# Fused attention and two expert layers: converted weight blocks used in place, q and k loads issued later, three small moves at the start

## Chip, cores and metric

One Trainium2 chip, one of its cores. The metric is the device time of one execution in microseconds (us), the median of three runs.

## The reference

Three stages follow each other: attention with a soft cap on the scores, a dense layer with a squared ReLU, and a top-1 expert layer.

```python
# q, k, v: (2 batches, 12 heads, 448 rows, 64), float32
s = q @ k.T / 8;  s = cap * tanh(s / cap);  a = exp(s - max) / (sum + 1e-9);  x = a @ v
# x becomes (896, 768); w_in (768, 2048) and w_out (2048, 768) are float64
x = relu(x @ w_in) ** 2 @ w_out
# 8 experts, w1 (8, 768, 1024), w2 (8, 1024, 768), float32
e = argmax(xn @ en.T / tau);  out = gate[e] * (relu(x @ w1[e]) @ w2[e])
```

## The kernel before

**Number format.** Every float32 operand of a big product is split into a high part in a reduced format and a low rest: `qh` and `ql` of a query, `kp` (both parts of a key stacked on the 128 partitions), `xh` and `xl` of the activations, `wh` and `wl` of a weight block. The dense layer then takes three products per block (lines 554 to 556).

**Attention.** The 24 heads are taken in pairs, m = 0 to 11. One pair is seven blocks of 128 keys: three of its first head, one that holds the last 64 keys of both, three of its second head. Two blocks make a group g. TensorE computes the scores `sc` of group g + 2 (line 423), ScalarE makes `p_t` of them by a tanh and an exponential (lines 425 and 426), and TensorE multiplies `p_t` of group g with the values (`pv`, line 444). Values lie in three rotating tiles `vt0`, `vt1`, `vt2` and, for the shared block, in `vs0` or `vs1`. A pair's result is divided on VectorE (`rs`, `rows`, lines 463 to 467), transposed on TensorE (`xp`, line 483), and split into `xh` (ScalarE) and `xl` (VectorE).

**Front of a head.** `turn(n)` transposes the loaded q and k of head n on VectorE into `tq`. `split_k` and `split_q` make `kp`, `qh` and `ql` of it; `ql` and the upper half of `qh` are GpSimd's. `front_first` is the same for head 0. `load_heads` loads q and k for the next pair with four transfers into `qk`, of which there are two; it is called in `turn` of each odd head, right behind the transpose that frees the tile.

**Weights.** w_in and w_out arrive as pairs of 32-bit words. A block's raw words are loaded into `wr` (768 KB, three buffers), scaled into `wf` (384 KB, four buffers) and patched with shifts (`narrow`, lines 205 to 208), then split into `wh` and `wl`. The first four blocks of w_in (NPRE) are converted during the attention of the first batch, by `convert_early`, one step of VectorE per group. Each is then stored to a buffer `wk` in DRAM, since the second batch reads all blocks there, and the first batch's dense layer loads it back from there (line 218) as block 0 to 3. Blocks 4 and on are scaled by ScalarE (line 222).

**Order.** All of it is one written order per engine. Loads, stores and reloads of the weights, q, k and v go through SyncE's queue (SP) alone, in program order; a transfer there also waits, as the program is built, for a transfer that stands some eight places before it. After the first batch's attention, mlp(0) is interleaved with the attention of the second batch.

Of the kernel before, what the change touches and what calls it, by code (L numbers as in the profile page):

```python
# [13 lines left out]
ALU = mybir.AluOpType  # L14
# [6 lines left out]
def kernel(  # L21
# [27 lines left out]
    nc = tc.nc  # L49
    f32 = lambda ap: ap.bitcast(F32)  # L50

    B, H, S, D = q.shape
# [3 lines left out]
    P = 128  # L56
# [35 lines left out]
    def load_heads():  # L92

        n = nload[0]
        if n >= len(order):
            return
        k_ = 1 if n < 2 else 2
        nload[0] = n + k_
        b, h = order[n]
        if n % 2 == 0:  # L100
            raw["tile"] = ap.tile([P, 2, S // SQ, SQ], F32, tag="qk", name=f"qk{n}", bufs=2)
        qk = raw["tile"][:, n % 2:n % 2 + k_].rearrange("p h s d -> p (h s) d")
        for i, a in enumerate((k, q)):
            halves = a[b].rearrange("h s d -> (h s) d")[h * S:(h + k_) * S].rearrange(
                "(s t) (j d) -> j t s d", t=SQ, d=SQ)
            for j in range(2):
                e = nc.scalar if n == 0 and j else nc.sync
                o = (2 * (1 - i) + j) * SQ
                e.dma_start(qk[o:o + SQ], halves[j])
        for i in range(k_):  # L110
            raw[n + i] = raw["tile"][:, n % 2 + i]

    def load_v(n, e=nc.sync):
        b, h = order[n]
        i = n % 2
        e.dma_start(vt[n % 3][:, :, :D], v[b, h, i * D:i * D + KS].rearrange("(c p) d -> p c d", p=P))
# [8 lines left out]


    capb = const.tile([P, 1], F32, name="capb")
    nc.scalar.dma_start(capb, cap.to_broadcast([P, 1]))
    load_v(0, nc.scalar)
    taub = const.tile([P, 1], F32, name="taub")  # L130

# [22 lines left out]
    def scale():  # L154
        nc.vector.reciprocal(rcap, capb)
        nc.vector.tensor_scalar_mul(rcap, rcap, 1.0 / (D ** 0.5))
# [18 lines left out]
    chunks = []  # L175
# [8 lines left out]
    def add_chunk(src, a, w, wide=False, keep=None, extra=False):  # L184
        chunks.append(dict(src=src, a=a, w=w, wide=wide, keep=keep, extra=extra))

    def w_tile(tag, n, c, bufs, dt=F32R):
        pool = extra_pool[n % 2] or wp
        bufs = bufs if pool is wp else 2
        t = pool.tile([P, WMAX], dt, tag=tag, name=f"{tag}{n}", bufs=bufs)  # L190
        return t[:, :c["a"] * c["w"]].rearrange("p (a w) -> p a w", a=c["a"])

    def raw_w(c, n):
        c["raw"] = ap.tile([P, 2 * WMAX], I32, tag="wr", name=f"wr{n}", bufs=3)[:, :2 * c["a"] * c["w"]].rearrange(
            "p (a w) -> p a w", a=c["a"])
        nc.sync.dma_start(c["raw"], c["src"]())
        c["parts"] = c["raw"].rearrange("p a (w t) -> p a w t", t=2)
# [14 lines left out]
    def w_stage(stage, n):  # L212

        c = chunks[n]

        def load():
            c["f"] = w_tile("wf", n, c, 4, F32)
            nc.sync.dma_start(c["f"], c["src"]())

        def scaled():  # L220
            c["f"] = w_tile("wf", n, c, 4, F32)
            nc.scalar.mul(c["f"], c["parts"][:, :, :, 1].bitcast(F32), 2.0 ** -112)
            c["narrow"] = narrow(c)

        def hi():
            c["hi"] = w_tile("wh", n, c, 4)
            if eng["hi"] == "act":
                nc.scalar.copy(c["hi"], c["f"])  # L228
            else:
                nc.vector.tensor_copy(c["hi"], c["f"])  # L230

        def lo():
            c["lo"] = w_tile("wl", n, c, 4)
            nc.vector.tensor_tensor(c["lo"], c["f"], f32(c["hi"]), op=ALU.subtract)  # L234

        if stage == "load" and c["wide"]:
            return [lambda: raw_w(c, n)]
        if stage == "conv0":
            return [scaled if c["wide"] else load]
        if stage == "conv1" and c["wide"]:  # L240
            return [lambda i=i: c["narrow"][i]() for i in range(3)]
        if stage == "store" and c["keep"] is not None:
            return [lambda: nc.sync.dma_start(c["keep"](), c["f"])]
        if stage == "split":
            return [hi, lo]
        return []
# [50 lines left out]
    early = []  # L297

    def convert_early():

        def first(i):
            c = early[i]
            c["f"] = w_tile("wf", 1000 + i, c, 4, F32)
            nc.vector.tensor_scalar_mul(c["f"], c["parts"][:, :, :, 1].bitcast(F32), 2.0 ** -112)
            c["narrow"] = narrow(c)

        def last(i):
            c = early[i]
            c["narrow"][2]()
            nc.sync.dma_start(c["keep"](), c["f"])  # L310
            if i + 2 < len(early):
                raw_w(early[i + 2], 1002 + i)

        for i in range(len(early)):
            yield first(i)
            yield early[i]["narrow"][0]()
            yield early[i]["narrow"][1]()
            yield last(i)

    def add_mlp_chunks(b):  # L320
        off = 0
        blocks = [(0, f, 0, NCC) for f in range(NF)]
        blocks += [(1, d, a, 4) for d in range(NCC) for a in range(0, NF, 4)]
        for m, col, a0, n in blocks:
            o = off

            def given(m=m, col=col, a0=a0, n=n):
                return w_src[m][a0 * P:(a0 + n) * P, col * P * wm:(col + 1) * P * wm].rearrange(
                    "(a p) w -> p a w", p=P)

            def kept(o=o, n=n):
                return wk[0][:, o:o + n * P].rearrange("p (a w) -> p a w", a=n)

            if not wide:
                add_chunk(given, n, P)
            elif b == 0 and m == 0 and col < NPRE:
                early.append(dict(src=given, a=n, w=P, keep=kept))
                add_chunk(kept, n, P)
            elif b == 0:
                add_chunk(given, n, P, True, kept)  # L340
            else:
                add_chunk(kept, n, P)
            off += n * P

    for b in range(B):
        add_mlp_chunks(b)
# [11 lines left out]
    def attention():  # L358
# [5 lines left out]
        def turn(n):  # L364

            qk = raw.pop(n)
            tq = ap.tile([P, S], F32, tag="tq", name=f"tq{n}", bufs=2)
            nc.vector.transpose(tq, qk.rearrange("p s d -> p (s d)"))
            if n % 2:
                load_heads()  # L370
            kp = ap.tile([P, S + D], F32R, tag="kp", name=f"kp{n}", bufs=3)
            i = n % 2
            nc.gpsimd.memset(f32(kp[:, :D] if i else kp[:, S:]), 0.0)
            qh = ap.tile([P, S], F32R, tag="qh", name=f"qh{n}", bufs=3)
            st[n] = (kp, qh, qlo[n % 3])
            front[n] = tq, kp[:, i * D:i * D + S], qh, qlo[n % 3]
# [7 lines left out]
        def split_q(n):  # L384

            tq, _, qh, ql = front[n]
            copy(qh[:D], tq[:D])
            nc.gpsimd.tensor_copy(qh[D:], tq[:D])
            nc.gpsimd.tensor_tensor(ql[D:], tq[:D], f32(qh[:D]), op=ALU.subtract)  # L389

        def front_first():

            turn(0)
            tq, keys, qh, ql = front[0]
            nc.scalar.copy(keys[D:], tq[D:])
            nc.vector.tensor_copy(qh[:D], tq[:D])
            nc.scalar.copy(qh[D:], tq[:D])
            nc.vector.tensor_tensor(keys[:D], tq[D:], f32(keys[D:]), op=ALU.subtract)  # L398
            nc.gpsimd.tensor_tensor(ql[D:], tq[:D], f32(qh[:D]), op=ALU.subtract)

        def copy(o, i):
            if eng["kh"] == "dve":
                nc.vector.tensor_copy(o, i)
            else:
                nc.scalar.copy(o, i)  # L405
# [81 lines left out]
        def fronts(g):  # L487

            for m, i in blocks[2 * g:2 * g + 2]:
                n = 2 * m + 2 + (i > 3)  # L490
                if i == 0 and n < N and not m:
                    turn(n)
                if i in (1, 5) and n < N:
                    split_k(n)
                    yield
                if i in (2, 6) and n < N:
                    split_q(n)
                    if n + 1 < N:
                        turn(n + 1)
                    yield  # L500
# [4 lines left out]

        todo, late, front = [], [], {}
        conv = convert_early()
        front_first()
        turn(1)
        scale()  # L510
        split_q(1)
        split_k(1)
        scores(0)
# [671 lines left out]
```

## Time and profile before

| | us |
|---|---|
| three runs | 522.92, 524.54, 525.24 |
| median | 524.54 |
| the profiled execution's own time | 524.37 |
| its span, first to last instruction | 522.6 |

| engine | busy us | share of the span |
|---|---|---|
| TensorE (PE) | 506.6 | 97% |
| VectorE (DVE) | 369.8 | 71% |
| ScalarE (ACT) | 283.2 | 54% |
| GpSimd (POOL) | 60.3 | 12% |

The span lies 1.77 us below the profiled execution's time; the rest lies around the instructions. All times in the rows below count from the start of the span. The first batch's attention fills about the first 77 us, mlp(0) with the second batch's attention goes to about 243 us, and what follows is mlp(1) and the experts.

### The profile page before, as it was taken

To read this page: it belongs to the slowest core of one execution; us is meant where nothing else is said; L and a number is where in the kernel's file an instruction comes from. 1 tells how busy PE (TensorE), PEld (TensorE's weight loads), DVE (VectorE), ACT (ScalarE), POOL (GpSimd) and SP (SyncE) were. 2 spreads that over 40 slices of the span, in tenths; PEclk is the share of its full clock that TensorE was granted. 3 is DMA by queue.
4 is the path that set the end of the run, shared out by engine and by line. 5 is a ranking of instruction groups with operands and counts; after the bars stand their busy time and mean duration, and the time that the engine had idled before them with its cause. 6 is when DMAs were issued, how large, how long until landed. Compare 5 with 4: busy or idle time off the path is not lost.

```text
span 522.6 us, 8325 instructions
## 1 busy us (share of the span) xinstructions
PE 506.6 (97%) x2898; PEld 464.4 (89%) x2898; DVE 369.8 (71%) x713; ACT 283.2 (54%) x521; POOL 60.3 (12%) x102
## 2 busy tenths in 40 slices
PE   7999979999999999999999999999999999999995
PEld 5899969999999999999998999999899898998993
DVE  6799969899998989765597476555358344446662
ACT  5978858687966787764244242222362323445531
POOL 5554431111120110002000000000000000000000
PEclk9999979999999999999999999999999999999998
DMA  8887996968855778765433123435512345544651
GB/s 123 191 170 172 226 259 187 232 202 268 207 180 181 222 237 249 229 208 155 159 117 121 43 74 110 135 124 153 156 44 78 108 137 170 184 156 151 213 151 40
DMA packets 129597, 85.19 MB, mean 163 GB/s; under 512 B 59010, under 2 KB 116226, under 8 KB 129552
## 3 DMA queue, kind: packets, MB, share of 16 engines
q1 hardware_dynamic: 119920, 79.07, 54.2%
q10 hardware_dynamic: 9536, 5.52, 4.0%
q8 instruction: 24, 0.39, 0.3%
q14 instruction: 21, 0.17, 0.1%
q0 software_dynamic: 96, 0.04, 0.0%
HBM read 66.68 MB, written 18.28 MB: 163 GB/s over the span
## 4 chain that ended last, share of the span: by engine, by line
PE 89%; DMA 5%; SPq 1%; DVE 1%; issue 1%; POOL 1%; ACT 0%; DVEq 0%; POOLq 0%; ACTq 0%
PE pv L444 9%; PE h L554 8%; PE y L554 8%; PE h L556 8%; PE h L555 7%; PE y L556 7%; PE y L555 7%; PE sc L423 5%; PE z L554 4%; PE e L554 4%; PE e L555 4%; PE z L556 4%; PE e L556 4%; PE z L555 4%; DMA vs<-in_v_dram 2%; DMA vt<-in_v_dram 2%
## 5 line engine op out<-in xcount | busy, mean ns | idle before, releaser
L234 DVE TENSOR_TENSOR wl<-wf,wh 128x512 fp32r<-128x512 f32 (+1 forms) x140 | 114.5, 830 | 48.1 <-ACT wh L228 46.8
L228 ACT CAST wh<-wf 128x512 fp32r<-128x512 f32 (+1 forms) x97 | 65.7, 697 | 20.4 <-PE z L556 8.8
L554 PE MATMUL y<-gh,wh 128*128 128x448 f32 x192 | 72.4, 377 | 0.0
L554 PE MATMUL h<-xh,wh 128*128 128x448 f32 x192 | 72.0, 375 | 0.0
L556 PE MATMUL h<-xl,wh 128*128 128x448 f32 x192 | 70.4, 367 | 0.0
L555 PE MATMUL h<-xh,wl 128*128 128x448 f32 x192 | 70.3, 366 | 0.0
L556 PE MATMUL y<-gl,wh 128*128 128x448 f32 x192 | 70.2, 366 | 0.0
L555 PE MATMUL y<-gh,wl 128*128 128x448 f32 x192 | 70.1, 365 | 0.0
L444 PEld LDWEIGHTS pv<-vt,p_t 128*112 128x112 f32 x576 | 64.4, 181 | 5.9 <-issue 4.1
L444 PE MATMUL pv<-vt,p_t 128*112 128x65 f32 x576 | 63.6, 262 | 3.8 <-DMA vt<-in_v_dram 3.8
L425 ACT ACTIVATE p_t<-sc,rcap 128x448 f32<-128x448 f32 x84 | 49.1, 631 | 21.5 <-PE sc L423 19.4
L426 ACT ACTIVATE p_t<-p_t,capb 128x896 f32<-128x896 f32 x42 | 43.9, 1045 | 1.4
L389 POOL TENSOR_TENSOR ql<-tq,qh 64x448 fp32r<-64x448 f32 x23 | 27.5, 1197 | 132.0 <-ACT qh L405 93.6
L584 ACT ACTIVATE r<-h 128x448 f32<-128x448 f32 x32 | 17.3, 540 | 45.0 <-PE h L556 32.4
L423 PE MATMUL sc<-qh,kp 128*128 128x448 f32 x96 | 37.2, 388 | 2.5 <-DVE kp L398 1.2
L230 DVE CAST wh<-wf 128x512 fp32r<-128x512 f32 (+1 forms) x43 | 21.9, 509 | 24.5 <-PE y L556 19.8
L556 PEld LDWEIGHTS h<-xl,wh 128*128 128x128 f32 x192 | 36.2, 188 | 3.1
L554 PEld LDWEIGHTS h<-xh,wh 128*128 128x128 f32 x192 | 36.3, 189 | 2.8
L556 PEld LDWEIGHTS y<-gl,wh 128*128 128x128 f32 x192 | 36.1, 188 | 3.0
L555 PEld LDWEIGHTS h<-xh,wl 128*128 128x128 f32 x192 | 36.3, 189 | 2.7
L555 PEld LDWEIGHTS y<-gh,wl 128*128 128x128 f32 x192 | 36.2, 188 | 2.5
L554 PEld LDWEIGHTS y<-gh,wh 128*128 128x128 f32 x192 | 36.1, 188 | 2.5
(239 smaller groups left out, 936.7 us busy)
## 6 DMA issues: line engine op xcount, KB each, us to landing
wr<-in_moe_w_in_dram SPq DMA_DIRECT2D x16, 768.0 KB, 5.4
wr<-in_moe_w_out_dram SPq DMA_DIRECT2D x24, 512.0 KB, 4.2
wf<-in_moe_w_dram SPq DMA_DIRECT2D x24, 384.0 KB, 3.5
wf<-in_moe_w_dram SPq DMA_DIRECT2D x36, 256.0 KB, 3.1
wf<-wk SPq DMA_DIRECT2D x20, 384.0 KB, 3.6
wk<-wf SPq DMA_DIRECT2D x16, 384.0 KB, 5.3
wk<-wf SPq DMA_DIRECT2D x24, 256.0 KB, 4.3
wf<-wk SPq DMA_DIRECT2D x24, 256.0 KB, 2.9
```

The lines of the kernel that those rows point to most:

```text
L228: nc.scalar.copy(c["hi"], c["f"])
L230: nc.vector.tensor_copy(c["hi"], c["f"])
L234: nc.vector.tensor_tensor(c["lo"], c["f"], f32(c["hi"]), op=ALU.subtract)
L389: nc.gpsimd.tensor_tensor(ql[D:], tq[:D], f32(qh[:D]), op=ALU.subtract)
L423: nc.tensor.matmul(sc[:, :S], h[0][:, c * P:(c + 1) * P], h[x], start=t == parts[0][0] and x == 1, stop=t == parts[-1][0] and x == 2)
L425: nc.scalar.activation(p_t[:, j], sc[:, :S], AF.Tanh, scale=rcap)
L426: nc.scalar.activation(p_t, p_t, AF.Exp, scale=capb)
L444: nc.tensor.matmul(o, w, x, start=i == 0 and t % 2 == 0, stop=i == NK - 1, skip_group_check=True)
L554: nc.tensor.matmul(o, wh, xh, start=first, stop=False)
L555: nc.tensor.matmul(o, wl, xh, start=False, stop=False)
L556: nc.tensor.matmul(o, wh, xl, start=False, stop=last)
L584: nc.scalar.activation(r, o[:, :S], AF.Relu)
```

## The change

Four things change; nothing else in the kernel does.

1. Blocks 0 to 3 take the converted tile `wf` as it lies (`taken`); their four reloads from `wk` are gone. Their stores to `wk` stay, each now issued one step later.
2. `load_heads` is called in block 6 of a pair, behind `split_q`, where it was in block 2 behind the transpose. The raw block that is fetched during the conversion is fetched at other steps.
3. The transfer of `cap` goes from ScalarE's queue to GpSimd's, and the two small operations of `scale` stand first on VectorE.
4. `ql` of head 0, and the upper half of `qh` of head 1, go from GpSimd to VectorE.

```diff
-    nc.scalar.dma_start(capb, cap.to_broadcast([P, 1]))
+    nc.gpsimd.dma_start(capb, cap.to_broadcast([P, 1]))
...
+        def taken():
+            c["f"] = c["early"]["f"]
+
+        if "early" in c and stage in ("load", "conv0"):
+            return [taken] if stage == "conv0" else []
...
-        def last(i):
-            c = early[i]
-            c["narrow"][2]()
-            nc.sync.dma_start(c["keep"](), c["f"])
-            if i + 2 < len(early):
-                raw_w(early[i + 2], 1002 + i)
+        def fetch(i):
+            if i < len(early):
+                raw_w(early[i], 1000 + i)
 
         for i in range(len(early)):
             yield first(i)
+            if i > 1:
+                fetch(i + 1)
             yield early[i]["narrow"][0]()
             yield early[i]["narrow"][1]()
-            yield last(i)
+            early[i]["narrow"][2]()
+            if not i:
+                fetch(2)
+            yield
+            nc.sync.dma_start(early[i]["keep"](), early[i]["f"])
...
-                add_chunk(kept, n, P)
+                add_chunk(None, n, P)
+                chunks[-1]["early"] = early[-1]
...
             nc.vector.transpose(tq, qk.rearrange("p s d -> p (s d)"))
-            if n % 2:
-                load_heads()
...
-            nc.gpsimd.tensor_copy(qh[D:], tq[:D])
+            (nc.gpsimd if n > 1 else nc.vector).tensor_copy(qh[D:], tq[:D])
...
-            nc.gpsimd.tensor_tensor(ql[D:], tq[:D], f32(qh[:D]), op=ALU.subtract)
+            nc.vector.tensor_tensor(ql[D:], tq[:D], f32(qh[:D]), op=ALU.subtract)
...
                     split_q(n)
+                    if i == 6:
+                        load_heads()
                     if n + 1 < N:
                         turn(n + 1)
...
+        scale()
         front_first()
         turn(1)
-        scale()
+        load_heads()
         split_q(1)
```

The order of instructions on TensorE does not change, and ScalarE's loses only the transfer. On VectorE the first rows change, those of heads 0 and 1. Before:

```order
L135 MEMSET zero_99 128x448
L368 STREAM_TRANSPOSE tq0_147<-qk0_86 128x448
L396 CAST qh0_151<-tq0_147 64x448
L398 TENSOR_TENSOR kp0_149<-tq0_147,kp0_149 64x448
L368 STREAM_TRANSPOSE tq1_157<-qk0_86 128x448
L155 RECIPROCAL rcap_134<-capb_95 128x1
L156 TENSOR_SCALAR rcap_134<-rcap_134 128x1
L403 CAST qh1_166<-tq1_157 64x448
L403 CAST kp1_164<-tq1_157 64x448
L382 TENSOR_TENSOR kp1_164<-tq1_157,kp1_164 64x448
L368 STREAM_TRANSPOSE tq2_196<-qk2_137 128x448
```

The same place on VectorE in the changed kernel:

```order
L135 MEMSET zero_99 128x448
L155 RECIPROCAL rcap_134<-capb_95 128x1
L156 TENSOR_SCALAR rcap_134<-rcap_134 128x1
L377 STREAM_TRANSPOSE tq0_149<-qk0_86 128x448
L403 CAST qh0_153<-tq0_149 64x448
L405 TENSOR_TENSOR kp0_151<-tq0_149,kp0_151 64x448
L406 TENSOR_TENSOR ql0_119<-tq0_149,qh0_153 64x448
L377 STREAM_TRANSPOSE tq1_159<-qk0_86 128x448
L410 CAST qh1_163<-tq1_159 64x448
L395 CAST qh1_163<-tq1_159 64x448
L410 CAST kp1_161<-tq1_159 64x448
L389 TENSOR_TENSOR kp1_161<-tq1_159,kp1_161 64x448
```

The two operations on `rcap` moved ahead of the first transpose, and `ql0` and the second part of `qh1` came over from GpSimd.

On SyncE's queue, in the program's order, this stands behind the first pairs' loads before the change (the number right behind `qk`, `vt` and `vs` is the head or tile, `wr1000` is the raw form of block 0):

```order
L109 DMA qk4_159<-in_k_dram 32x28x32 x2
L109 DMA qk4_159<-in_q_dram 32x28x32 x2
L109 DMA qk6_208<-in_k_dram 32x28x32 x2
L109 DMA qk6_208<-in_q_dram 32x28x32 x2
L116 DMA vt2_83<-in_v_dram 128x3x64
L196 DMA wr1000_217<-in_moe_w_in_dram 128x6x256
L196 DMA wr1001_219<-in_moe_w_in_dram 128x6x256
L121 DMA vs1_85<-in_v_dram 64x64 x2
L116 DMA vt0_81<-in_v_dram 128x3x64
```

And this in the changed kernel:

```order
L109 DMA qk4_164<-in_k_dram 32x28x32 x2
L109 DMA qk4_164<-in_q_dram 32x28x32 x2
L116 DMA vt2_83<-in_v_dram 128x3x64
L196 DMA wr1000_212<-in_moe_w_in_dram 128x6x256
L196 DMA wr1001_214<-in_moe_w_in_dram 128x6x256
L109 DMA qk6_255<-in_k_dram 32x28x32 x2
L109 DMA qk6_255<-in_q_dram 32x28x32 x2
L121 DMA vs1_85<-in_v_dram 64x64 x2
L116 DMA vt0_81<-in_v_dram 128x3x64
```

The four transfers of q and k for heads 6 and 7 moved behind the two raw blocks.

The second place on the same queue is the end of the first batch's attention. Before:

```order
L116 DMA vt2_83<-in_v_dram 128x3x64
L196 DMA wr4_743<-in_moe_w_in_dram 128x6x256
L218 DMA wf1_745<-wk_136 128x768
L109 DMA qk16_766<-in_k_dram 32x28x32 x2
L109 DMA qk16_766<-in_q_dram 32x28x32 x2
L196 DMA wr5_806<-in_moe_w_in_dram 128x6x256
L218 DMA wf2_808<-wk_136 128x768
L310 DMA wk_136<-wf1003_712 128x768
L116 DMA vt0_81<-in_v_dram 128x3x64
L121 DMA vs0_84<-in_v_dram 64x64 x2
L196 DMA wr6_849<-in_moe_w_in_dram 128x6x256
L218 DMA wf3_861<-wk_136 128x768
```

And in the changed kernel:

```order
L116 DMA vt2_83<-in_v_dram 128x3x64
L196 DMA wr4_741<-in_moe_w_in_dram 128x6x256
L196 DMA wr5_797<-in_moe_w_in_dram 128x6x256
L109 DMA qk16_821<-in_k_dram 32x28x32 x2
L109 DMA qk16_821<-in_q_dram 32x28x32 x2
L116 DMA vt0_81<-in_v_dram 128x3x64
L121 DMA vs0_84<-in_v_dram 64x64 x2
L196 DMA wr6_842<-in_moe_w_in_dram 128x6x256
L326 DMA wk_136<-wf1003_705 128x768
```

The reloads `wf1`, `wf2`, `wf3` are gone, `wr5` moved ahead of the four transfers of q and k, and the store of block 3 moved from ahead of `vt0` to behind it.

## Rows read from the trace of the kernel before

**Rows 1.** TensorE's waits, 5 to 75 us: total us, times, longest.

```profile
PE pv L444 <- DMA vt<-in_v_dram: 3.8, 1, 3.8
PE pv L444 <- DMA vs<-in_v_dram: 1.6, 1, 1.6
```

**Rows 2.** Stretches: length, busy PE, PEld, DVE, ACT, POOL, PEclk, DMA share, GB/s.

```profile
26.00:69.50 43.50, 42.50 (x346) 40.80 (x346) 42.32 (x79) 36.28 (x51) 21.87 (x28) 1.00 0.91 200
69.50:73.30 3.80, 0.05 (x1) 0.08 (x1) 3.61 (x9) 2.32 (x4) 1.70 (x2) 0.79 0.93 301
73.30:78.50 5.20, 5.20 (x24) 5.06 (x25) 0.69 (x2) 1.91 (x3) 0.00 (x0) 0.50 1.01 184
...
100.00:243.00 143.00, 143.00 (x866) 133.50 (x865) 124.11 (x214) 106.25 (x199) 16.85 (x30) 1.00 0.73 217
```

**Rows 3.** Timeline of TensorE, end of the first attention: start, duration, instruction.

```profile
76.26 0.95 PE L483 MATMUL xp<-ident,rows 112*128 112x112 f32 x4
```

**Rows 4.** Timeline of VectorE, the same place.

```profile
68.20 0.63 DVE L368 STREAM_TRANSPOSE tq<-qk 128x448 f32<-128x448 f32 x1
...
71.44 0.76 DVE L467 TENSOR_TENSOR rows<-pv,rs 112x256 f32<-112x256 f32 x2
...
72.66 0.62 DVE L382 TENSOR_TENSOR kp<-tq,kp 64x448 fp32r<-64x448 f32 x1
77.81 0.62 DVE L485 TENSOR_TENSOR xl<-xp,xh 128x448 fp32r<-128x448 f32 x1 [4.54 <-ACT xh L484]
```

**Rows 5.** Timeline of SyncE's queue, the same place.

```profile
63.21 0.74 SPq L196 DMA_DIRECT2D wr<-in_moe_w_in_dram  x1
...
64.72 0.38 SPq L310 DMA_DIRECT2D wk<-wf  x1
65.19 0.38 SPq L116 DMA_DIRECT2D vt<-in_v_dram  x1
```

**Rows 6.** The chain that ended last, near 65 us: start, length, what.

```profile
65.19 7.92 DMA vt<-in_v_dram
```

**Rows 7.** Timeline of all engines, the first 12 us.

```profile
4.57 0.65 DVE L368 STREAM_TRANSPOSE tq<-qk 128x448 f32<-128x448 f32 x1 [3.16 <-DMA qk<-in_q_dram]
...
5.79 1.12 POOL L399 TENSOR_TENSOR ql<-tq,qh 64x448 fp32r<-64x448 f32 x1 [1.89 <-DVE qh L396]
...
5.84 1.55 DVE L398 TENSOR_TENSOR kp<-tq,kp 64x448 fp32r<-64x448 f32 x1 [0.21 <-ACT kp L395]
...
9.30 1.45 DVE L382 TENSOR_TENSOR kp<-tq,kp 64x448 fp32r<-64x448 f32 x1
...
10.77 0.65 DVE L368 STREAM_TRANSPOSE tq<-qk 128x448 f32<-128x448 f32 x1
```

**Rows 8.** Timeline of all engines, 20 to 23 us.

```profile
20.02 1.69 PE L444 MATMUL pv<-vt,p_t 128*112 128x65 f32 x16
...
22.19 0.56 DVE L304 TENSOR_SCALAR wf<-wr 128x768 f32<-128x768 f32 x1 [2.42 <-DMA wr<-in_moe_w_in_dram]
...
22.67 0.35 DVE L463 TENSOR_SCALAR rs<-pv,ecap 112x4 f32<-112x4 f32 x2
```

**Rows 9.** Timeline of SyncE's queue, 10 to 27 us.

```profile
10.03 1.21 SPq L109 DMA_DIRECT2D qk<-in_q_dram  x2
...
16.63 1.07 SPq L196 DMA_DIRECT2D wr<-in_moe_w_in_dram  x2
...
19.99 2.74 SPq L109 DMA_DIRECT2D qk<-in_k_dram  x2
22.78 4.10 SPq L109 DMA_DIRECT2D qk<-in_q_dram  x2
```

**Rows 10.** Transfers by line: issues, KB each, median us from issue to landing.

```profile
qk<-in_q_dram SPq DMA_DIRECT2D x22, 112.0 KB, 3.8
...
taub<-in_moe_tau_dram ACTq DMA_DIRECT2D x1, 0.5 KB, 5.9
xg<-x2d,ixu POOLq DMA_INDIRECT x1, 3.1
```

## The prediction

> **What bounds the kernel now.** I read the stretches first, then TensorE's waits, then the timelines at the places that the two name.
>
> From 100 to 243 us TensorE is busy throughout at full clock, VectorE 124.11 of 143 us [rows 2]. There a change of loads is worth nothing by itself; what counts is how early TensorE gets there. Before that the stretches show two things. From 26 to 69.5 us TensorE has 42.50 of 43.50 us and VectorE 42.32: both are full, and neither can go ahead of the other for long. Then comes a hole: from 69.5 to 73.3 us TensorE does nothing, and from 73.3 to 78.5 us it works at a granted clock of 0.50, the 1.2 GHz level, where the rows around show 1.00, the 2.4 GHz level [rows 2].
>
> The waits say what made the hole: `pv` stood 3.8 us for a load of `vt`, the longest wait of the attention; the next one, 1.6 us for `vs`, lies near 25 us [rows 1]. The chain of waits shows that load: issued at 65.19 us, 7.92 us until it has landed [rows 6]. SyncE wasn't late with it. Just ahead in its queue stand a raw block (768 KB, 63.21 us), a reload of a converted block (384 KB) and a store (384 KB, 64.72 us) [rows 5], and the load landed behind them.
>
> So the hole costs 3.8 us of standing and, at half clock, half of the 5.2 us after it, 2.6 us: 6.4 us in all.
>
> **The hole.** The change takes the three reloads `wf1` to `wf3` from this place and a fourth one ahead of it, moves the store behind `vt0`, and puts both raw blocks, `wr4` and `wr5`, ahead of the four transfers of q and k. `vt0` then has 1.5 MB of raw blocks ahead, as much as today in all, but they needn't wait for a transpose any more and can be under way earlier. `vt0` itself can't be issued before TensorE's last read of the tile. That lies three groups ahead of the use at 69.5 us; a group is 2.5 us (8.8 us a pair, below), with its own reading some 9 us: 60.5 us on today's clock, 59 with the advance below. So its issue lies between 59 and today's 65.19, and I take 60, near the lower end, as what stood ahead of it is gone or earlier. Even with the 7.92 us of now it lands at 68. TensorE will want it at 69.5 − 2.4 = 67.1 (below), so it is at worst 0.9 us late, and that hides in the next wait. I take the wait as gone.
>
> **What is late next.** Behind this `pv` TensorE transposes `rows` (`xp`), and VectorE writes them at 71.44 to 72.20 us [rows 4]. VectorE didn't stand in the hole, it caught up. So `xp`, now at 76.26 us [rows 3], can't come before 72.25 on today's clock of VectorE: 76.26 − 72.25 = 4.0 us, not 6.4. From `xp` to 78.5 us are 2.24 us at half clock, of which 1.1 come back if the clock stays up. The stand that is left, about 2 us, is near the 1.6 us at `vs`, after which the clock stands at 1.00 [rows 1, 2], and further from 3.8. VectorE then no longer stands 4.54 us for `xh` [rows 4], so it moves up with TensorE.
>
> **VectorE's own advance.** The hole's new end moves with VectorE, so what VectorE gains ahead counts in full. Two places:
>
> *The start.* The low part of key 0 takes 1.55 us beside GpSimd's `ql` of 1.12 us, that of key 1 1.45 us, where the same operation takes 0.62 elsewhere [rows 4, 7]. With `ql0` on VectorE (about 0.65, like that 0.62) the first drops to 0.62; the second still meets GpSimd's `ql1`, at about 0.85. The upper half of `qh1` adds 0.4; the two operations of `scale` leave their place behind the second transpose (0.3) and go where VectorE waits 3.16 us for q [rows 7]. Sum: −0.93 + 0.65 − 0.6 + 0.4 − 0.3 = −0.8 us up to the transpose at 10.77. Bounds: if the contention stays, −0.93 and −0.6 fall away and it is +0.75.
>
> *The first raw block.* VectorE waits 2.42 us for it until 22.19 us [rows 8]; it was issued at 16.63, behind q and k of heads 6 and 7, which wait for a transpose. SyncE has nothing to do from 11.24 us on [rows 9], and now `vt2` and the raw blocks stand next: issue at about 12, landing 4.6 us earlier, at 17.6, ahead of VectorE, which is free at 22.19 − 2.42 − 0.8 = 19.0. It then stands for TensorE instead: the `pv` at 20.02 lasts 1.69 us [rows 8], less 0.8 gives 20.9 for `rs`, which is at 22.67 now. The advance is 1.7 us from there on (about 2.4 + 0.8 if nothing stood in the way, 0.8 if the block came no earlier).
>
> TensorE's 1.6 us at `vs` goes too, as `vs1` is issued some 2 us earlier behind raw blocks 4.6 us earlier. That gives nothing more: VectorE sets the pace, and TensorE's lead of 2.4 us turns into the stand before `xp`.
>
> **Edits at nothing.** `cap`: the nearest rows are 3.1 us from issue to landing for the one gather on GpSimd's queue and 5.9 us for `tau`, a load of the same size [rows 10]. GpSimd can issue it near 0.8 us; I take 3.1, landing at 3.9, hidden behind q at 4.57, as it is the row of that queue. At 5.9 it would be 6.7, and VectorE's first transpose would start at 7.0: 2.4 us lost. The stores one step later, the raw block fetched at another step: nobody waits for them within a group. Taking the tile in place adds no instruction; ScalarE needs the tile again only for block 4, after VectorE has split block 0.
>
> **Sum.** 1.7 + 4.0 + 1.1 = 6.8 us against the profiled execution's 524.37 us: 517.6 us. That execution is 0.17 us below the median, which I neglect. The 1.77 us around the span stay.
>
> **Rivals.**
>
> *TensorE isn't held by VectorE.* If the timeline slides together better than I read it, the whole 6.4 come back, and TensorE's 0.8 + 1.6: 8.8 us, 515.6. For it: VectorE's durations vary with what GpSimd does beside them. Against: 42.32 of 43.50 [rows 2].
>
> *The hole moves and stays.* `vt0` still stands behind 1.5 MB of raw blocks. If it is late by more than the 2 us that VectorE allows, TensorE stands as long as now and the clock falls again. Then only the 1.7 us of advance are left: 522.7, no change that can be told. For it: `vt` took 7.92 us behind 1.5 MB. Against: the earlier issue.
>
> *`cap` comes late.* VectorE's first row waits for it. By the 5.9 us above: 517.6 + 2.4 = 520.0. The Trainium skill speaks for this one (SBUF — State Buffer, section "SBUF: two separate sides"): descriptors of a transfer issued by GpSimd are written through the port pair that it shares with VectorE, and such a transfer went from about 620 to about 3100 ns beside a VectorE copy. No run here shows it yet; in the first microseconds VectorE has one memset.
>
> *q and k come late (slower).* A pair of heads takes, by the transposes of heads 2 and 15, (68.20 − 10.77) ÷ 13 × 2 = 8.8 us [rows 4, 7]. The loads had 11 of 7 blocks from call to transpose, 13.9 us, and now have 7, 8.8 us. Behind the two raw blocks, the load of now was issued from 19.99 to 26.88 us [rows 9] and lands 3.8 us later [rows 10]: 10.7 us. If each of the five pairs up to the hole took that, VectorE would wait 1.9 us five times, 9.5 us: 517.6 + 9.5 = 527.1. It is slower than now from 1.4 us late each. Against: one pair alone stands behind two raw blocks in the new order, and the 6.9 us of issuing were spent waiting for transfers that will have landed earlier. The Trainium skill bears on it (DMA: Bandwidth & Descriptors, section "Queues, rings and completion order"): each DMA engine takes a queue's descriptors in order, so small loads behind big ones wait; the `vt` load agrees, at 7.92 us behind 1.5 MB [rows 5, 6].
>
> **Chances and range.** Forecast 0.56; TensorE free 0.15; hole stays 0.14; `cap` late 0.08; q and k late 0.06; 0.01 for the rest. About 0.5%, 2.6 us, is what a measurement of this kernel can tell from no change. Faster than that: the forecast, the first and the third rival, and a quarter of the second, 0.83; same 0.11; slower 0.06. The range runs from just under the free TensorE, 515.0, to 522.0, which takes in the late `cap` and a hole that stays in part. Alone, the forecast would have 516 to 519.
>
> **What would show it.** In the profile after: no wait of TensorE near 67 us over 2.5 us; granted clock 1.00 from 12 us to 243 us; `xp` before block 0's first matmul held by `rows` of VectorE; no wait of VectorE for a raw block; `rcap` written before the first transpose, which starts at 4.6; the transpose of head 2 near 10.0; the mlp's first matmul 6 to 7 us earlier. I am wrong if VectorE waits for q and k at any of the transposes, if `vt` or `vs` still holds TensorE long enough for 0.50 to show up, or if the lead is lost between 100 and 243 us.

## The result, and the profile after

The changed kernel takes 518.33 us (median of 5 executions, 517.87 to 520.11) against 524.54 us (522.92 to 525.32): a ratio of 0.9899, 95% interval 0.987 to 0.9927. Six more executions of it gave 518.25 us, 0.9878 (0.9851 to 0.9904). Predicted were 517.6 us. The profiled execution took 517.91 us, 6.46 less than the profiled one of before (524.37), with a span of 516.2 us.

The stretches, with the columns of [rows 2]:

```profile
26.00:66.00 40.00, 40.00 (x331) 38.82 (x330) 39.00 (x75) 35.44 (x51) 20.41 (x26) 1.00 0.86 181
66.00:70.00 4.00, 3.30 (x30) 2.92 (x29) 3.93 (x8) 3.93 (x6) 2.85 (x3) 1.00 0.46 72
70.00:74.00 4.00, 3.75 (x23) 3.35 (x22) 3.83 (x9) 2.82 (x6) 0.00 (x0) 1.00 0.95 306
74.00:78.00 4.00, 4.00 (x29) 3.76 (x29) 4.00 (x5) 4.00 (x7) 1.60 (x2) 1.00 0.24 35
...
100.00:243.00 143.00, 143.00 (x862) 133.36 (x861) 121.08 (x208) 105.58 (x202) 17.19 (x30) 1.00 0.76 218
```

The hole is gone: TensorE loses 0.7 us between 66 and 70 us and 0.25 behind it, and the granted clock stays at 1.00, where [rows 2] have 3.75 us of standing and 5.2 us at 0.50. TensorE's waits from 3 to 100 us say the same (columns as in [rows 1]):

```profile
PE sc L430 <- DVE kp L389: 1.5, 1, 1.5
...
PE pv L451 <- DMA vt<-in_v_dram: 0.7, 1, 0.7
PE xp L490 <- DVE rows L474: 0.2, 1, 0.2
```

The 3.8 us for `vt` are 0.7, the 1.6 us for `vs` are gone. The timeline of TensorE at that place:

```profile
68.66 1.76 PE L451 MATMUL pv<-vt,p_t 128*112 128x65 f32 x16 [0.70 <-DMA vt<-in_v_dram]
70.66 0.65 PE L490 MATMUL xp<-ident,rows 112*128 112x112 f32 x4 [0.25 <-DVE rows L474]
```

`xp` stood at 76.26 us [rows 3]: it is 5.60 us earlier, and what releases it is VectorE's `rows`. The timeline of VectorE, at the start, at the first raw block and at the end of the first attention:

```profile
4.83 0.17 DVE L155 RECIPROCAL rcap<-capb 128x1 f32<-128x1 f32 x1 [3.41 <-DMA capb<-in_cap_dram]
...
5.21 0.65 DVE L377 STREAM_TRANSPOSE tq<-qk 128x448 f32<-128x448 f32 x1
...
6.48 0.62 DVE L405 TENSOR_TENSOR kp<-tq,kp 64x448 fp32r<-64x448 f32 x1 [0.21 <-ACT kp L402]
7.14 0.62 DVE L406 TENSOR_TENSOR ql<-tq,qh 64x448 fp32r<-64x448 f32 x1
...
9.28 1.24 DVE L410 CAST kp<-tq 64x448 fp32r<-64x448 f32 x1
10.55 0.62 DVE L389 TENSOR_TENSOR kp<-tq,kp 64x448 fp32r<-64x448 f32 x1
11.21 0.65 DVE L377 STREAM_TRANSPOSE tq<-qk 128x448 f32<-128x448 f32 x1
...
20.13 1.37 DVE L309 TENSOR_SCALAR wf<-wr 128x768 f32<-128x768 f32 x1
21.43 0.34 DVE L470 TENSOR_SCALAR rs<-pv,ecap 112x4 f32<-112x4 f32 x2
...
68.60 0.96 DVE L234 TENSOR_TENSOR wl<-wf,wh 128x768 fp32r<-128x768 f32 x1
69.47 0.35 DVE L470 TENSOR_SCALAR rs<-pv,ecap 112x4 f32<-112x4 f32 x2
...
70.09 0.76 DVE L474 TENSOR_TENSOR rows<-pv,rs 112x256 f32<-112x256 f32 x2
...
71.95 0.62 DVE L492 TENSOR_TENSOR xl<-xp,xh 128x448 fp32r<-128x448 f32 x1
```

VectorE starts later than before: `rcap` waits 3.41 us for `capb`, the first transpose is at 5.21 us instead of 4.57, that of head 2 at 11.21 instead of 10.77 [rows 7]. At the first raw block it no longer waits, and `rs` is at 21.43 us instead of 22.67 [rows 8]. From then on it is 1.24 to 1.36 us ahead (`rows` 70.09 against 71.44, [rows 4]), and `xl` follows at once, where it stood 4.54 us. The conversion of the block itself takes 1.37 us, where [rows 8] have 0.56, and GpSimd's timeline has a `ql` beside it:

```profile
19.73 1.36 POOL L396 TENSOR_TENSOR ql<-tq,qh 64x448 fp32r<-64x448 f32 x1 [0.33 <-DVE qh L410]
```

The timeline of SyncE's queue:

```profile
11.95 1.07 SPq L196 DMA_DIRECT2D wr<-in_moe_w_in_dram  x2
...
56.59 1.07 SPq L196 DMA_DIRECT2D wr<-in_moe_w_in_dram  x2
57.76 3.26 SPq L109 DMA_DIRECT2D qk<-in_k_dram  x2
61.07 3.57 SPq L109 DMA_DIRECT2D qk<-in_q_dram  x2
64.73 1.86 SPq L116 DMA_DIRECT2D vt<-in_v_dram  x1
```

The first raw blocks are issued 4.7 us earlier than in [rows 9]. `vt0` is issued at 64.73 us, only 0.46 earlier than in [rows 5], but it has landed by 68.66, in 3.9 us instead of 7.92 [rows 6].

### The profile page after: what moved, and what is told of

Read it like the earlier page. It is cut to its first block, busy times and chain, and to the rows that moved or that the text cites. A ratio compares the mean times of both kernels' runs of the same rounds, so it can differ in the third digit from the quotient of the medians.

```text
span 516.2 us, 8318 instructions
## 1 busy us (share of the span) xinstructions
PE 504.6 (98%) x2898; PEld 462.1 (90%) x2898; DVE 369.6 (72%) x715; ACT 282.8 (55%) x521; POOL 62.4 (12%) x101
## 4 chain that ended last, share of the span: by engine, by line
PE 85%; DVE 10%; DMA 1%; issue 1%; ACT 1%; DVEq 0%; ACTq 0%; POOLq 0%
PE h L564 8%; PE y L564 8%; PE h L566 8%; PE h L565 8%; PE y L566 8%; PE y L565 8%; PE pv L451 6%; PE z L564 4%; PE e L564 4%; PE e L565 4%; PE e L566 4%; PE z L566 4%; PE z L565 4%; PE sc L430 3%; DVE tq L377 2%; DVE kp L410 1%
## 5 line engine op out<-in xcount | busy, mean ns | idle before, releaser
L451 PEld LDWEIGHTS pv<-vt,p_t 128*112 128x112 f32 x576 | 63.0, 178 | 3.0 <-PE sc L430 1.0
L451 PE MATMUL pv<-vt,p_t 128*112 128x65 f32 x576 | 62.2, 259 | 0.7 <-DMA vt<-in_v_dram 0.7
L396 POOL TENSOR_TENSOR ql<-tq,qh 64x448 fp32r<-64x448 f32 x23 | 27.8, 1210 | 126.8 <-ACT qh L412 67.1
```

The lines of the kernel that those rows point to most:

```text
L451: nc.tensor.matmul(o, w, x, start=i == 0 and t % 2 == 0, stop=i == NK - 1, skip_group_check=True)
```

## The experiments

Each has five rounds beside runs of the kernel before on the same chip; ratios are to that kernel, with the 95% interval. The four kernels with one raw block less or with the store ahead ran on another chip than the other experiments. A profile shows one execution. Medians of kernels near 518 us scatter by about 1 us, so below that the verdicts rest on rows.

**Part one alone.** The kernel before, with the reloads dropped and the tiles used where they lie; store, q and k, raw blocks and start as before.

```diff
+        def taken():
+            c["f"] = c["early"]["f"]
+
+        if "early" in c and stage in ("load", "conv0"):
+            return [taken] if stage == "conv0" else []
...
-                add_chunk(kept, n, P)
+                add_chunk(None, n, P)
+                chunks[-1]["early"] = early[-1]
```

> The kernel before with only the first part of the change: blocks used where they lie, no reloads; q, k, the store, the raw blocks and the start as before. Theory: without the reloads vt0 is issued and landed in time or up to 1 us late, VectorE still waits 2.4 us for the first raw block, so the result is that of the run with the old order of q and k: 520. Rival (the store and the raw block issued just ahead of vt0 hold it as much as the reloads did): wait over 2.5 us, clock 0.50, 522 to 524.

Measured: 519.07 us, 0.9892 (0.9868 to 0.9915); the profiled execution 518.83. Its timelines, SyncE's queue, TensorE and VectorE:

```profile
63.59 0.38 SPq L116 DMA_DIRECT2D vt<-in_v_dram  x1
```

```profile
69.54 1.76 PE L450 MATMUL pv<-vt,p_t 128*112 128x65 f32 x16 [0.16 <-DMA vt<-in_v_dram]
71.95 0.65 PE L489 MATMUL xp<-ident,rows 112*128 112x112 f32 x4 [0.65 <-DVE rows L473]
```

```profile
21.85 0.56 DVE L309 TENSOR_SCALAR wf<-wr 128x768 f32<-128x768 f32 x1 [2.16 <-DMA wr<-in_moe_w_in_dram]
```

This part alone removes the hole: 0.16 us of wait for `vt0`, `xp` at 71.95, held by `rows`. The prediction had 72.25 as the earliest on VectorE's clock of before. Between the profiled executions it is 5.54 us, of the 6.46 of the whole change. VectorE still waits for the first raw block. The rival (store and raw block hold `vt0` as much) falls.

**The rest without part one.** The changed kernel with the reloads and the store back ahead of `vt0`.

```diff
-                add_chunk(None, n, P)
-                chunks[-1]["early"] = early[-1]
+                add_chunk(kept, n, P)
...
-            yield
             nc.sync.dma_start(early[i]["keep"](), early[i]["f"])
+            yield
```

> The four reloads of converted blocks and the store ahead of vt0 are back; q, k and the start stay as changed. Theory (what stood ahead of vt0 made the hole): pv near 68 us waits 3 to 4 us for vt0 again, granted clock 0.50 behind it, the hole's 4.0 + 1.1 us come back: 523.0. Rival (issuing q and k later was what removed it): no wait over 1 us there, 518.

Measured: 525.36 us over 12 executions, 1.0003 (0.998 to 1.0026): the whole gain is gone. SyncE's queue, TensorE, and the stretch behind:

```profile
63.68 6.15 SPq L109 DMA_DIRECT2D qk<-in_q_dram  x2
69.93 0.49 SPq L116 DMA_DIRECT2D vt<-in_v_dram  x1
```

```profile
72.50 3.22 PE L450 MATMUL pv<-vt,p_t 128*112 128x65 f32 x16 [4.70 <-DMA vt<-in_v_dram]
```

```profile
70.00:74.00 4.00, 1.50 (x8) 1.53 (x9) 1.72 (x4) 2.44 (x4) 0.00 (x0) 0.56 0.56 97
```

VectorE has its lead here too (`rows` at 69.96 us), and it buys nothing, since TensorE stands 4.70 us for `vt0`. SyncE needs 6.15 us to issue the last two transfers of q behind the raw blocks and reloads, and `vt0` stands behind them. The median is 2.4 above the expected 523.0. I had put the hole at its size of before, but here both raw blocks, two reloads and the store come ahead of q and k, and the wait is longer than the 3.8 of before. That explains a part at most: the profiled execution, with this wait, took 523.52 us, 0.5 above the expected; the other eleven go up to 528.0, and what they lost has no trace.

**One store, or one raw block less.** The changed kernel with only the store back ahead of `vt0` (the last piece of the diff above), and with only one raw block ahead of it:

```diff
-    AHEAD = {"load": 6 + NRAW, "conv0": 6, "conv1": 5, "store": 4, "split": 3}
+    AHEAD = {"load": 5 + NRAW, "conv0": 6, "conv1": 5, "store": 4, "split": 3}
```

> Only the store of the fourth block is back ahead of vt0 (384 KB more ahead; the reloads, 1.1 MB more, brought pv's wait from 0.70 to 4.70 us). Theory (the wait goes by the bytes ahead): vt0 comes about 1 us later, pv waits 1.7 us, of which VectorE's rows hide 0.25; 519.0, and 520.5 if the clock falls at that wait as it did at 1.24 us in the run with the old start. Rival (reloads delay for another reason, such as reading what was just stored): no change, 518.

> The changed kernel with the raw block wr5 fetched one step later, which puts it behind vt0: vt0 has one raw block (768 KB) ahead instead of two. Theory (vt0 is held by what stands ahead of it in SyncE's queue, and after it VectorE sets the pace): vt0 is issued near 61 us, pv near 68 us no longer waits, but rows and xp stay where VectorE has them (70.1 and 70.7 us in a run whose clock was 1.00 before), so the time stays within 0.5 of 517.9; it may fall to half clock less often. Rival (TensorE alone sets the pace there): xp comes 0.7 us earlier, 517.2.

Measured with the store: 519.54 us, 0.9912 (0.9892 to 0.9933), the profiled execution 517.96: the wait for `vt0` is 1.12 us instead of 0.70, the clock stays at 1.00, `xp` is at 70.56. So 384 KB cost 0.4 us there and not 1. With one raw block: 519.51 us, 0.991 (0.9888 to 0.9932), and no wait for `vt0`. Four kernels with the same order of q and k thus give the issue of `vt0` by what lies between the first raw block and it, q and k apart:

| raw blocks, reloads, store ahead | KB | issue of `vt0`, us |
|---|---|---|
| one raw block | 768 | 61.96 |
| two (the changed kernel) | 1536 | 64.73 |
| two and the store | 1920 | 65.23 |
| two, the store, two reloads | 2688 | 69.93 |

The issue comes later with more bytes ahead, 8.0 us over 1920 KB, but not in proportion. Counted from the issue of the first raw block (56.01, 56.59, 56.46 and 57.77 us) it comes 5.95, 8.14, 8.77 and 12.16 us later: one more raw block, 768 KB, adds 2.2 us, the store, 384 KB, 0.6 and the two reloads, again 768 KB, 3.4. So the rival that reloads delay for a further reason than their bytes isn't ruled out. The run with one raw block shows something else, in VectorE's timeline and in TensorE's:

```profile
68.41 0.34 DVE L470 TENSOR_SCALAR rs<-pv,ecap 112x4 f32<-112x4 f32 x2
...
69.02 0.76 DVE L474 TENSOR_TENSOR rows<-pv,rs 112x256 f32<-112x256 f32 x2
69.69 0.95 DVE L234 TENSOR_TENSOR wl<-wf,wh 128x768 fp32r<-128x768 f32 x1
```

```profile
69.59 0.65 PE L490 MATMUL xp<-ident,rows 112*128 112x112 f32 x4 [0.23 <-DVE rows L474]
...
97.03 0.97 PE L451 MATMUL pv<-vt,p_t 128*112 128x65 f32 x8 [2.10 <-issue]
```

The step that moved took `wl` (0.95 us) from ahead of `rs` to behind `rows`, and `xp` came 1.07 us earlier, of which 0.13 are an earlier start: `xp` follows VectorE there, one for one. I had expected `xp` to stay put; it moved for the reason of the theory and not of the rival. The lead is lost again at 97 us, where TensorE stands 2.10 us. The trace names no releaser, but the times point to VectorE: this `pv` takes the two banks that VectorE's `rows` reads just before, and it starts 0.52 us behind the start of `rows` (96.51 us). The distance is 0.52 to 0.53 us in all six runs that stand at this `pv`, for 0.16 to 2.10 us. The changed kernel has it too, with no stand (`rows` 95.45, `pv` 95.98 us), and part one alone has not (95.52 and 97.07). So what TensorE gains ahead of this place beyond the changed kernel is lost here unless `rows` comes earlier as well; no run moves that `rows` alone.

**q and k at their old place.** The changed kernel with `load_heads()` behind every odd transpose again.

```diff
+            if n % 2:
+                load_heads()
...
-                    if i == 6:
-                        load_heads()
```

> Only the issue of q and k is back at its old place, behind every odd transpose; blocks are still used where they lie. Theory: the first raw block is issued near 16.6 us again and VectorE waits for it near 20 us, so its advance of about 1.7 us from there is gone; vt0 has no reload ahead but raw blocks that are issued late, so it may still be late by 1 to 3 us. 519.6 if the hole stays away, 522 if it is back in part. Rival (the reloads were everything, the order of q and k nothing): 518.3 and no wait of VectorE for the raw block.

Measured: 520.16 us, 0.9911 (0.9888 to 0.9935). VectorE and TensorE:

```profile
23.38 0.56 DVE L309 TENSOR_SCALAR wf<-wr 128x768 f32<-128x768 f32 x1 [3.27 <-DMA wr<-in_moe_w_in_dram]
```

```profile
73.07 0.65 PE L492 MATMUL xp<-ident,rows 112*128 112x112 f32 x4 [1.29 <-DVE rows L476]
```

As expected VectorE waits for the raw block, which is issued at 17.04 us, and `rs` is at 23.85 instead of 21.43. Against the changed kernel it costs 1.8 us; with the old start the move is worth less: `rs` is at 22.32 us in part one alone, which has the old order too, against 21.00 in the run with the old start below, 1.3 us where it is 2.4 here. (Their medians, 519.07 and 518.64, are too close to tell.) `vt0` holds nobody, so against the expectation the hole doesn't come back in part: the raw blocks alone don't make it.

**The start.** The changed kernel with the start of before; with cap on ScalarE's queue and one raw block less ahead of `vt0`; and with the old start and one raw block less. The first of them:

```diff
-    nc.gpsimd.dma_start(capb, cap.to_broadcast([P, 1]))
+    nc.scalar.dma_start(capb, cap.to_broadcast([P, 1]))
...
-            (nc.gpsimd if n > 1 else nc.vector).tensor_copy(qh[D:], tq[:D])
+            nc.gpsimd.tensor_copy(qh[D:], tq[:D])
...
-            nc.vector.tensor_tensor(ql[D:], tq[:D], f32(qh[:D]), op=ALU.subtract)
+            nc.gpsimd.tensor_tensor(ql[D:], tq[:D], f32(qh[:D]), op=ALU.subtract)
...
-        scale()
         front_first()
         turn(1)
+        scale()
```

> Only the start is as before: cap on ScalarE's queue, scale behind the second transpose, qh1's upper half and ql0 on GpSimd. Theory by the profile after: the transpose of head 2 comes 0.44 us earlier (10.77 against 11.21), since rcap doesn't wait 3.4 us for GpSimd's transfer, and VectorE sets the pace up to 72 us: 517.9 (0.4 less than the changed kernel). Rival (the start's parts are worth the 0.8 us of the prediction): the transpose near 12.0 and 519.1.

> wr5 behind vt0, and cap on ScalarE's queue; the rest of the changed start stays. By the profile after, cap on GpSimd's queue delays the first transpose by 0.64 us, and the rest of the start gains 0.20. Theory: first transpose at 4.6 if cap lands by then (in before it was needed only at 8.0, so this isn't known; ScalarE issues it at 1.84 us behind two loads of head 0), transpose of head 2 at 10.6, 517.3. Rival (cap lands as late on this queue): transpose of head 2 at 11.2 and 517.9.

> wr5 behind vt0 and the start of before (cap on ScalarE's queue, scale behind the second transpose, qh1's upper half and ql0 on GpSimd). In the run with the old start alone VectorE was 0.44 us ahead, but pv stood 1.24 us for vt0 and the clock was 0.58 for 4 us behind it. Theory: with vt0 out of the way the 0.44 us come through and the clock holds: 517.5, pv without a wait, granted clock 1.00 from 70 to 78 us. Rival (the old start costs something else): 518.6 again.

Measured: old start 518.64 us, 0.9877 (0.9848 to 0.9907); cap on ScalarE's queue 520.25, 0.9916 (0.9897 to 0.9935); old start with one raw block less 519.35, 0.9914 (0.9887 to 0.9942), the profiled execution 517.89. With the old start the transpose of head 2 is at 10.77 us, as expected, and `rows` 0.40 us earlier; but TensorE then stands for `vt0` (timeline), and the clock falls (stretch):

```profile
68.74 1.76 PE L451 MATMUL pv<-vt,p_t 128*112 128x65 f32 x16 [1.24 <-DMA vt<-in_v_dram]
```

```profile
70.00:74.00 4.00, 4.00 (x19) 3.65 (x18) 3.78 (x8) 2.28 (x4) 0.00 (x0) 0.58 0.90 288
```

So VectorE's 0.4 us turn into a wait for the load, and the margin at `vt0` is that thin. Cap on ScalarE's queue, VectorE's timeline:

```profile
4.77 0.16 DVE L155 RECIPROCAL rcap<-capb 128x1 f32<-128x1 f32 x1 [3.35 <-DMA capb<-in_cap_dram]
```

It lands as late from that queue, issued at 1.84 us, as from GpSimd's, issued at 1.36. My theory of the queue falls: `cap` is late because `scale` now stands ahead of the first transpose. The trace of the kernel before has it already, in its transfers by line (columns as in [rows 10]):

```profile
capb<-in_cap_dram ACTq DMA_DIRECT2D x1, 0.5 KB, 3.1
```

Issued at 1.84 us there too, it landed at 4.9 us, behind the first transpose at 4.57, when nobody needed it yet. Most of this run's time is lost where one raw block less costs it, before 100 us: TensorE is busy 14.07 of the 16 us from 84 us on, with a stand of 1.93 us at 96.84, and the clock falls behind it (stretch):

```profile
98.00:102.00 4.00, 4.00 (x14) 3.55 (x13) 3.93 (x6) 2.83 (x4) 0.00 (x0) 0.58 0.34 54
```

The old start with one raw block less has 0.19 us of wait for `vt0` and clock 1.00 from 70 to 78 us, as expected, and loses the gain at the same place, 1.27 us at 95.89.

**`vt0` from another queue.** v of head 12 issued by GpSimd, in the changed kernel, in that with `scale` behind the second transpose, and in the kernel before.

```diff
-                    load_v(2 * m + 2)
+                    load_v(2 * m + 2, nc.gpsimd if m == 5 else nc.sync)
```

> The changed kernel with one load taken out of SyncE's queue: v of head 12 (vt0 near 65 us, the one that TensorE waits for) is issued by GpSimd. Theory (it is late because SyncE is still held at the transfers of heads 16 and 17): issue near 62 us instead of 64.7, pv without a wait near 68 us; xp stays where VectorE's rows have it (70.1 us, by the start of that run), so the median stays at 518 and only runs that lost the clock there gain. Rival (the DMA engines are full, not the queue): it lands no earlier than 68.6.

> As the run before, and scale back behind the second transpose, so that VectorE's first transpose doesn't wait for cap; cap stays on GpSimd's queue, ql0 and qh1's upper half stay on VectorE. In two runs cap landed at 4.7 us from either queue, so its place in the program decides and not its queue. Theory: first transpose at 4.6, that of head 2 at 10.7 (10.77 in before, 11.1 to 11.2 in the changed kernel), rows and xp 0.4 us earlier, 517.5. Rival: the contention moves once more and head 2 comes at 11.1 or later; 518.

> The kernel before with nothing changed but v of head 12 issued by GpSimd. If the hole alone (the load's wait and the half clock behind it) is most of what the change removed, this gets the terms of the hole, 4.0 + 1.1 us, without any other part: 519.4 against 524.5, xp near 72.3 instead of 76.3, clock 1.00. Rival (the load is late since the DMA engines are busy with reloads and raw blocks, so another queue doesn't help): still 2 us or more of wait, 522 or more.

Measured: 518.08 us, 0.9872 (0.9847 to 0.9896); 518.16, 0.9872 (0.9846 to 0.9897); and for the kernel before 524.26 over 12 executions, 0.9969 (0.9943 to 0.9994). GpSimd's and TensorE's timelines, first in the changed kernel, then in the kernel before:

```profile
63.30 0.77 POOL L116 DMA_DIRECT2D vt<-in_v_dram  x1
```

```profile
68.76 1.76 PE L451 MATMUL pv<-vt,p_t 128*112 128x65 f32 x16 [1.07 <-DMA vt<-in_v_dram]
```

```profile
66.83 0.96 POOL L116 DMA_DIRECT2D vt<-in_v_dram  x1
```

```profile
74.00 1.89 PE L444 MATMUL pv<-vt,p_t 128*112 128x65 f32 x16 [2.65 <-DMA vt<-in_v_dram]
```

In the changed kernel the load is issued 1.4 us earlier and has landed at the same time, near 68.6 us. So there the rival holds: it is the transfers in flight that delay `vt0`, and not SyncE's queue alone. In the kernel before it takes 7.0 us from GpSimd's queue, beside the reloads and raw blocks, where it took 7.92 from SyncE's [rows 6]; GpSimd itself comes to it late, at 66.83, behind a wait for VectorE. The median there is far from the expected 519.4 and near the rival's, but the run settles less than the other. Its profiled execution had lost 1.9 us before the hole (the `pv` ahead of it is at 68.79 us instead of 66.90): TensorE stood 1.92 us for `vs` instead of 1.6, and the clock fell behind it (timeline and stretch):

```profile
27.30 1.66 PE L444 MATMUL pv<-vs,p_t 128*112 128x130 f32 x8 [1.92 <-DMA vs<-in_v_dram]
```

```profile
28.00:30.00 2.00, 2.00 (x13) 2.00 (x11) 1.95 (x4) 0.00 (x0) 0.24 (x1) 0.50 0.61 111
```

And two of the twelve executions took 519.21 and 520.20 us, near the 519.4; they have no trace. So how much this one move can give in the kernel before stays open. With `scale` back, head 2 is transposed 6.11 us after the first transpose (6.20 before, 6.00 in the changed kernel), and it comes at 10.96 us, since q lands only at 4.85 in that execution; of the 0.4 us expected, 0.25 show at this transpose, and at 96.25 us TensorE stands 0.48 us behind `rows`. Neither kernel can be told from the changed one; no version here beats it.

**The changed kernel again.**

> The changed kernel once more, for the scatter of its runs and as the ground for the next three. If the load of vt0 is only just in time (it stood TensorE still for 0.7 us in the first profile), some runs should lose the clock again: times between 517.9 and about 520, median near 518.3. If the scatter has another cause, the profile shows clock 1.00 to 243 us whatever the time.

Measured: 518.25 us (517.83 to 520.91). The profiled execution took 519.50 us, 1.6 more than the first profile, and its wait for `vt0` is 0.56 us at clock 1.00. It lost the time at the start, by its stretches and by VectorE's timeline:

```profile
8.00:10.00 2.00, 2.00 (x7) 1.28 (x6) 1.92 (x4) 1.73 (x3) 1.13 (x1) 0.60 0.62 94
10.00:12.00 2.00, 0.96 (x3) 0.81 (x3) 1.90 (x4) 0.99 (x2) 0.56 (x3) 0.50 1.04 164
12.00:14.00 2.00, 2.00 (x8) 1.78 (x8) 1.94 (x4) 1.66 (x3) 1.04 (x2) 0.50 1.16 151
```

```profile
22.61 0.22 DVE L470 TENSOR_SCALAR rs<-pv,ecap 112x4 f32<-112x4 f32 x1 [1.26 <-PE pv L451]
```

From 8 to 14 us TensorE works at a granted clock of 0.50 to 0.60, and VectorE then waits 1.26 us for `pv`. The first profile has 1.00 in all these stretches. So what this execution lost comes from the clock at the start, not from `vt0`: my expectation named the wrong place for it. The other executions have no trace.

## Why the prediction was right, point by point

- **The hole (4.0 + 1.1 us): right, and shown.** Part one alone gives 5.54 us between profiled executions, with `xp` 4.31 us earlier and the clock at 1.00. Without part one nothing of the gain is left. That `rows` on VectorE is what comes next is shown by `wl`, whose 0.95 us moved `xp` by as much. The reason given for the clock, that it would bear a stand of about 2 us, was not put to the test: 0.70 and 0.25 us were left. Other runs lost the clock behind 1.24, 1.92 and 1.93 us and kept it behind 2.10, so whether it had held behind 2 us is open, and that less was left is luck.
- **How `vt0` comes in time: right in effect, wrong in the step.** I had it issued at 60 us and still 7.92 us under way. It was issued at 64.73, since SyncE took 6.9 us to issue q and k behind the raw blocks, and landed in 3.9 us. The two errors cancel, which is luck: 68 predicted, 68.66 measured. TensorE wanted it at 67.96 us and not at 67.1, which kept the wait at 0.70.
- **VectorE's advance (1.7 us): mis-sized in both halves.** The start was to give 0.8 and costs 0.44. `cap` is the larger part: I priced it by the gather's row and by `tau`'s, passed over its own (3.1 us behind an issue at 1.84) and put GpSimd's issue at 0.8 us, which was 1.36. I had it landed at 3.9 us, it came at 4.83, and with `scale` ahead the first transpose is 0.64 us late. Behind it the edits give 0.20: the low part of key 0 fell from 1.55 to 0.62 us and `ql0` took 0.62 on VectorE, as predicted; the low part of key 1 fell to 0.62 too, but its cast rose from 0.64 to 1.24 us, so the contention with GpSimd moved by one operation. The first raw block gave 1.7 us instead of 0.9, and not by the path forecast: `rs` was to stand for TensorE's `pv`, but follows VectorE's own conversion, 0.81 us longer beside GpSimd's `ql`. Together 1.24 us at `rs`, 1.29 at `xp` against part one alone, and 0.92 at the end of the profiled executions. Of the 0.4 us between, 0.2 are gone at the `pv` near 97 us (95.98 against 97.07, a lead of 1.09), where the changed kernel comes up to VectorE's `rows`; the rest I did not follow. The sum by measured terms is 5.54 + 0.92 = 6.46, predicted 6.8.
- **The rivals.** TensorE free of VectorE: no, `xp` waits for `rows`. The hole stays: no, though near; with VectorE 0.44 us earlier the wait is 1.24 us and the clock falls. q and k late: VectorE waits for none of them. `cap` late: yes, by 0.64 us instead of the 2.4 priced. The Trainium skill (SBUF — State Buffer, "SBUF: two separate sides") spoke for it by descriptors that GpSimd writes beside VectorE; the runs give no sign of that, as `cap` lands at 4.74 us from ScalarE's queue too. The Trainium skill (DMA: Bandwidth & Descriptors, "Queues, rings and completion order") says that each DMA engine takes a queue's descriptors in order, from which I had small loads wait behind big ones of their queue. The table above fits that, but in the profiled executions the load from GpSimd's queue took 5.3 us beside the raw blocks and 7.0 beside the reloads too: leaving the queue didn't free it.

## What to carry to other kernels

When a small load ends a wait of the bound engine, count the bytes in flight ahead of it on all queues, and drop transfers before reordering them: here the reloads, 384 KB each, were worth 5.5 us, and the reordering around them nothing while they stayed. Then ask which engine is next (here VectorE's `rows`), since it caps the gain, and look for the next place where the two meet: with one raw block less, a lead won at 70 us was lost at 97. An edit that removes contention at the start of a stage needs its neighbours priced as well: the second engine's work meets the next operation instead.

## What the runs showed that I had not expected

- The length of a stand alone doesn't tell what the clock does behind it: behind 1.24 us (old start) the granted clock was 0.58 for 4 us and behind 1.93 us (cap on ScalarE's queue) too, but it stayed at 1.00 behind 1.12 us (with the store), 1.6 (`vs`, before) and 2.10 us (one raw block).
- The clock was at 0.50 to 0.60 from 8 to 14 us in one execution and at 1.00 in another of the same kernel, which costs 1.46 us at `rows` (71.55 against 70.09 us) and 1.6 at the end. In the run with the store it was 0.50 to 0.71 from 8 to 12 us, and `rows`, at 69.99, came no later for it.
- SyncE's issue of two transfers of 112 KB (q for heads 16 and 17) took 2.48 to 6.15 us behind raw blocks and reloads, where [rows 9] have 1.21 us at 10.03 us. The bytes ahead alone don't set it: 4.05 us behind one raw block, 3.57 behind two, 2.48 behind two and the store, 6.15 with two reloads besides.
